# A linear-attention and SwiGLU kernel: the eps of the norm in a 385th column, another ring for 237 PSUM tiles, and a new order of its steps

## The chip, the cores and the metric

The kernel runs on one core of one Trainium2 chip. The metric is the device time of one execution in microseconds (us), as the median of several runs. A profile of one execution stands beside it; its times are from the span's start. In the profile, PE is TensorE, PEld its weight loads, DVE is VectorE, ACT is ScalarE, POOL is GpSimd and SP is SyncE, which here only issues DMA transfers (SPq).

## The reference

Batch 4, 8 heads, 768 tokens, 48 columns per head. The first half is a linear attention whose state decays per token and column; its output, 3072 rows of 384, goes through an RMS norm with a gain and a SwiGLU block of width 1536.

```python
for t in range(S):
    cur = np.einsum('bhd,bhe->bhde', u[None] * kt, vt)
    y[:, :, t] = np.einsum('bhd,bhde->bhe', rt, state + cur)
    state = wt[:, :, :, None] * state + np.einsum('bhd,bhe->bhde', kt, vt)
...
rms = np.sqrt(np.mean(x * x, axis=-1, keepdims=True) + 1e-06)
xn = x / rms * rms_g
g = xn @ w_gate
silu = g * (1.0 / (1.0 + np.exp(-g)))
val = xn @ w_val
return (silu * val @ w_out).astype(np.float32)
```

## The kernel before

Tokens are worked in blocks of 128. There are six blocks (n = 0 to 5) of four batches (j = 0 to 3). Blocks 0 and 1 are loaded together (384 KB for each input and batch) and handled as pairs of interleaved tokens; blocks 2 to 5 come in loads of 192 KB. Each piece of work is a small function, a step, called as `name.n.j`.

The steps of one block and batch, in the order of their data: `load_w`, `load_k`, `load_r`, `load_v` (SP, L248 for the first two blocks, L258 later); `ln` of the decay (ACT); running sums on PE (`cs_mm`, `cs_k`) and `cs_add` (DVE); `exp_r` and `exp_k` (ACT); the products `r_mul` (DVE) and `k_mul` (POOL L457, the "k product"); `bonus_mul`, two products on POOL (L464, L465), their sum `bonus_sum` (DVE L469) and `bonus_v` (POOL L475, the "v product"); the transpose of r and k, which blocks 0 and 1 do on PE (`rk_pe`, L482) with a copy on DVE or ACT (`rk_tr`), and blocks 2 to 5 by a transposing DMA on SP (`rk_tr`, L487); the score product `q_mm` (PE L501 to L515, two batches at a time from block 2 on), its masks `q_mask_e` and `q_copy_o`, and for some batches a select on POOL, `q_mask_o` (L536); `cast_v` (ACT or POOL L384); the state (`st_mm`, `st_new`) and the output `y_mm`; `x_add`, `x_sq` (L581), `x_rstd`, `xn_mul` for the norm; a transpose, `xn_pe` and `xn_out`, or for blocks 4 and 5 `xn_tr` (SP) and `xn_gain` (POOL L625). Then the block's feed-forward: twelve units each of `gate_mm` and `val_mm` (PE L646), `silu` (ACT), `h_mul` (DVE L666, the gating product), then `o_mm` (PE L683, the output product), `o_out` and `out_dma` (SP L707). `warm` (L377) is a dummy matmul on zeros.

POOL also issues the weight transfers, which cast on the way: `load_gv.1.0` and `load_gv.1.1` are eight of the twelve column blocks of the gate and the value weights (768 KB as they land), `load_gv.0.0` and `load_gv.0.1` the other four, and `load_wo` (L353) the output weights. The first value unit in both orders uses the large value transfer.

The order is written out: `ORDER` is a table of all steps, and every engine runs its own steps in the order in which they stand there. An engine that waits for one step holds all of its later steps. Sets of names (`CAST_ACT`, `XN_DVE`, `RK_DVE`, `ODD_DVE`, `RSTD_ACT`, `OUT_DVE`) choose the engine of single steps.

PSUM's eight banks are three rings: a (2 banks, default for gate units and running sums), b (2, value units) and q (4, all else). `psum()` (L225) takes in a ring the free bank whose last use in the table lies furthest back. ACT holds one of two tables of functions; `act()` (L234) puts a table load (L236) ahead of a step that needs the other one: logarithm and exponential, or silu.

Of the kernel before, what the change touches and what calls it, by code (L numbers as in the profile page):

```python
# [10 lines left out]
FP32 = mybir.dt.float32  # L11
# [25 lines left out]
bonus_v.1.0 exp_k.0.3 exp_r.0.3 y_mm.0.0 warm.23.0 q_mm.0.5 warm.24.0 warm.25.2 x_add.0.0 q_copy_o.0.5 y_mm.1.0
q_mask_o.0.5 cast_v.1.1 q_mask_e.0.5 cast_v.0.1 load_v.0.2 r_mul.0.2 x_sq.0.0 x_add.1.0 rk_pe.1.2 load_w.2.0
load_w.2.1 rk_tr.1.2 q_mm.0.1 warm.26.0 warm.27.0 warm.28.0 warm.29.2 q_copy_o.0.1 q_mask_e.0.1 exp_r.1.3 load_gv.1.1
q_mm.1.1 warm.30.2 x_rstd.0.0 st_mm.0.0 k_mul.0.2 w_tot.0.2 x_sq.1.0 q_mask_e.1.1 xn_mul.0.0 load_v.0.3 bonus_v.0.1  # L40
x_rstd.1.0 y_mm.0.1 rk_pe.0.2 q_copy_o.1.1 load_w.2.3 w_tot.0.3 xn_pe.0.0 st_new.0.0 xn_mul.1.0 x_add.0.1 cs_k.0.3
rk_tr.0.2 exp_k.1.3 xn_out.0.0 x_sq.0.1 bonus_mul.1.1 r_mul.0.3 xn_pe.1.0 warm.31.1 warm.32.2 xn_out.1.0 q_mm.1.5
warm.33.1 gate_mm.0.2 silu.0.2 gate_mm.0.3 silu.0.3 q_mask_o.1.1 q_mask_e.1.5 x_rstd.0.1 bonus_sum.1.1 q_copy_o.1.5
q_mm.1.2 r_mul.1.3 load_r.2.0 k_mul.1.3 bonus_v.1.1 bonus_mul.0.3 y_mm.1.1 xn_mul.0.1 x_add.1.1 gate_mm.0.5
gate_mm.0.4 q_mm.1.6 q_mask_e.1.2 load_gv.0.0 k_mul.0.3 q_copy_o.1.2 q_mask_e.1.6 silu.0.5 load_gv.0.1 bonus_mul.1.2
rk_pe.1.3 rk_tr.1.3 val_mm.0.3 xn_pe.0.1 xn_out.0.1 h_mul.0.3 q_copy_o.1.6 x_sq.1.1 val_mm.0.5 x_rstd.1.1 q_mm.1.7
# [87 lines left out]
def kernel(  # L134
# [610 lines left out]
```

## Time and profile before

| | us |
|---|---|
| median of 3 runs | 200.35 |
| lowest and highest of them | 199.78, 203.26 |
| span of the profiled execution | 197.6 |

The profiled execution is one execution by itself; what the page gives of it is its span, from the first to the last instruction. In the page, the share behind an engine is its busy time over the span. Of the transfers that the change moves, these are some (the last column is the median of us from issue to landing):

```profile
out_dram<-ob SPq DMA_DIRECT2D x19, 192.0 KB, 2.4
wt<-in_w_dram SPq DMA_DIRECT2D x16, 192.0 KB, 4.2
...
wt<-in_w_dram SPq DMA_DIRECT2D x4, 384.0 KB, 4.3
rt<-in_r_dram SPq DMA_DIRECT2D x4, 384.0 KB, 4.9
kt<-in_k_dram SPq DMA_DIRECT2D x4, 384.0 KB, 4.9
...
wo_sb<-in_moe_w_out_dram POOLq DMA_DIRECT2D x3, 384.0 KB, 7.1
```

A line such as `wt<-in_w_dram` reads "tile from tensor".

### The profile page before, as it was taken

Reading aid. Unit: us, or ns where it says so; the run is one execution under the profiler, and the core shown is the slowest. Engines: PE = TensorE matmul, PEld = TensorE weight load, DVE = VectorE, ACT = ScalarE, POOL = GpSimd, SP = SyncE. Lnnn points to the kernel's source line nnn. Section 1 sums busy time; section 2 is a strip of 40 time slices with the busy share of each in tenths; the row PEclk is TensorE's granted clock in tenths of the full one; section 3 lists DMA queues with packets and bytes.
Section 4 is the critical chain, followed back from the end, with each engine's and each line's share of the span. In section 5 each row is a group of like instructions: output and inputs, shape, how many; then the busy total and the mean of one; then the engine's idle time right before and its main releaser. Section 6 shows DMA issues by size and latency. Waiting matters only on the chain.

```text
span 197.6 us, 4751 instructions
## 1 busy us (share of the span) xinstructions
PE 191.5 (97%) x1742; PEld 120.4 (61%) x1742; DVE 156.4 (79%) x315; ACT 139.1 (70%) x286; POOL 127.5 (64%) x181
## 2 busy tenths in 40 slices
PE   7899999999999999999999999999999999999994
PEld 3456677888665556655655655666655655555563
DVE  5699998999997999989799988997689842435530
ACT  3989998979997889795699875698556760514201
POOL 3399999988599759793969998599661544000000
PEclk9999999999999999999999999999999999999999
DMA  6999999999897999999999967924580021012112
GB/s 164 320 325 267 244 220 205 220 213 197 174 230 162 199 179 214 200 211 214 185 206 225 202 147 166 227 51 145 134 216 12 5 60 60 20 63 80 40 60 101
DMA packets 109807, 32.42 MB, mean 164 GB/s; under 512 B 104276, under 2 KB 108632, under 8 KB 109784
## 3 DMA queue, kind: packets, MB, share of 16 engines
q1 hardware_dynamic: 107744, 28.58, 63.4%
q0 software_dynamic: 2032, 3.54, 10.0%
q8 instruction: 13, 0.21, 0.5%
q14 instruction: 10, 0.08, 0.1%
q10 hardware_dynamic: 8, 0.00, 0.0%
HBM read 25.96 MB, written 4.72 MB: 155 GB/s over the span
## 4 chain that ended last, share of the span: by engine, by line
PE 83%; DMA 7%; POOL 6%; SPq 1%; issue 1%; ACT 0%; POOLq 0%
PE ps_bu L646 13%; PE ps_bv L646 12%; PE ps_av L646 11%; PE ps_au L646 11%; PE ps_qv L683 7%; PE ps_qx L683 6%; PE ps_qz L683 6%; DMA wv_sb<-in_moe_w_val_dram 5%; PE ps_qu L683 5%; DMA kt<-in_k_dram 2%; POOL ruk L464 1%; POOL ruk L465 1%; SPq L248 1%; POOL qts L536 1%; PE ps_qz L513 1%
## 5 line engine op out<-in xcount | busy, mean ns | idle before, releaser
L238 ACT ACTIVATE sg<-ps_av 128x512 bf16<-128x512 f32 x36 | 21.5, 596 | 27.1 <-PE ps_av L646 21.4
L683 PEld LDWEIGHTS <-ht 128*128 128x128 bf16 x312 | 28.6, 98 | 18.3 <-DVE ht L666 0.4
L646 PEld LDWEIGHTS <-wg_sb 128*128 128x128 bf16 x252 | 27.0, 114 | 16.6 <-issue 0.3
L646 PEld LDWEIGHTS <-wv_sb 128*128 128x128 bf16 x252 | 26.4, 114 | 16.0 <-DMA wv_sb<-in_moe_w_val_dram 0.7
L666 DVE TENSOR_TENSOR ht<-ps_bu,sg 128x512 bf16<-128x512 f32 x37 | 25.4, 687 | 10.7 <-PE ps_bu L646 8.3
L666 DVE TENSOR_TENSOR ht<-ps_bv,sg 128x512 bf16<-128x512 f32 x35 | 24.0, 686 | 9.9 <-PE ps_bv L646 8.5
L646 PE MATMUL ps_bu<-xnt,wv_sb 128*128 128x512 bf16 (+1 forms) x135 | 30.3, 343 | 0.5 <-DMA wv_sb<-in_moe_w_val_dram 0.5
L646 PE MATMUL ps_av<-xnt,wg_sb 128*128 128x512 bf16 (+1 forms) x126 | 29.4, 350 | 0.0
L646 PE MATMUL ps_au<-xnt,wg_sb 128*128 128x512 bf16 (+1 forms) x126 | 29.3, 349 | 0.1
L646 PE MATMUL ps_bv<-xnt,wv_sb 128*128 128x512 bf16 (+1 forms) x117 | 28.5, 358 | 0.0
L464 POOL TENSOR_TENSOR ruk<-rt,kt 128x384 f32<-128x384 f32 x24 | 24.0, 1002 | 1.9 <-DVE diag L469 1.4
L465 POOL TENSOR_TENSOR ruk<-ruk,u_bc 128x384 f32<-128x384 f32 x24 | 24.0, 1000 | 1.9
L238 ACT ACTIVATE sg<-ps_au 128x512 bf16<-128x512 f32 x36 | 21.5, 596 | 4.5 <-PE ps_au L646 3.3
L457 POOL TENSOR_TENSOR rk<-kt,ek 128x384 bf16<-128x384 f32 x20 | 19.8, 1001 | 6.6 <-DMA kt<-in_k_dram 5.5
L475 POOL TENSOR_TENSOR ydiag<-vt,diag 128x384 f32<-128x384 f32 x24 | 19.9, 836 | 1.0 <-DVE diag L469 1.0
L236 ACT ACT_TABLE_LOAD x14 | 18.0, 1283 | 1.9 <-PEq L729 1.6
L536 POOL TENSOR_SCALAR_AFFINE_SELECT qts<-qts 128x512 bf16<-128x512 bf16 x19 | 11.9, 637 | 11.2 <-ACT qts L533 8.0
L683 PE MATMUL ps_qv<-wo_sb,ht 128*128 128x384 bf16 (+1 forms) x96 | 15.5, 311 | 0.0
L581 ACT ACTIVATE junk<-xb 128x384 bf16<-128x384 f32 x24 | 12.5, 521 | 4.2 <-DVE xb L576 3.9
L469 DVE TENSOR_REDUCE diag<-ruk 128x8 f32<-128x384 f32 x24 | 13.0, 544 | 0.0
L683 PE MATMUL ps_qx<-wo_sb,ht 128*128 128x384 bf16 x72 | 12.7, 326 | 0.0
L683 PE MATMUL ps_qz<-wo_sb,ht 128*128 128x384 bf16 x72 | 12.7, 326 | 0.0
(212 smaller groups left out, 376.8 us busy)
## 6 DMA issues: line engine op xcount, KB each, us to landing
out_dram<-ob SPq DMA_DIRECT2D x19, 192.0 KB, 2.4
wt<-in_w_dram SPq DMA_DIRECT2D x16, 192.0 KB, 4.2
rt<-in_r_dram SPq DMA_DIRECT2D x16, 192.0 KB, 4.4
vt<-in_v_dram SPq DMA_DIRECT2D x16, 192.0 KB, 3.7
kt<-in_k_dram SPq DMA_DIRECT2D x16, 192.0 KB, 4.0
wt<-in_w_dram SPq DMA_DIRECT2D x4, 384.0 KB, 4.3
rt<-in_r_dram SPq DMA_DIRECT2D x4, 384.0 KB, 4.9
kt<-in_k_dram SPq DMA_DIRECT2D x4, 384.0 KB, 4.9
```

The lines of the kernel that those rows point to most:

```text
L236: nc.scalar.preload_act_table_set(table_name)
L238: return nc.scalar.activation(**kw).ins
L457: eng.tensor_tensor(out=rk[:, n % 2, j, 1, :, 0:D], in0=inp["k", n, j], in1=bank["cs_k", n, j][:, 0:DM].rearrange("p (h d) -> p h d", h=H) ...
L464: eng.tensor_tensor(out=ruk[n, j], in0=inp["r", n, j], in1=inp["k", n, j], op=ALU.mult)
L465: eng.tensor_tensor(out=ruk[n, j], in0=ruk[n, j], in1=u_bc, op=ALU.mult)
L469: nc.vector.tensor_reduce(out=diag[n, j].rearrange("p h o -> p (h o)"), in_=ruk[n, j], axis=mybir.AxisListType.X, op=ALU.add)
L475: eng.tensor_tensor(out=ydiag[n, j], in0=inp["v", n, j], in1=diag[n, j].to_broadcast([128, H, D]), op=ALU.mult)
L536: nc.gpsimd.affine_select(out=qts[n, j][:, 1], in_=qts[n, j][:, 1], compare_op=ALU.is_ge if n < 2 and j // 4 < n else ALU.is_gt, fill=0.0, ...
L581: nc.scalar.activation(out=junk, in_=xb[n, j], func=AF.Square, accum_out=rstd[n, j][:, 0:1])
L646: nc.tensor.matmul(ps.rearrange("p (i t) -> p i t", t=cols.stop - cols.start)[:, i, :], lhsT=units(ws, c, fs.start + i), rhs=xnt[n][:, c, ...
L666: nc.vector.tensor_tensor(out=ht[n][:, fs, cols], in0=bank.pop(("v", n, f)).rearrange("p (i t) -> p i t", i=fs.stop - fs.start), in1=bank. ...
L683: nc.tensor.matmul(ps[:, cols], lhsT=ht[n][:, f, b * L:(b + 1) * L], rhs=wo_sb[:, f, cols], start=(f == 0), stop=(f == FC - 1))
```

## The change

Four things are done.

1. **The eps column.** The sum x that the norm works on was a tile of 384 columns. It now lies in one of four rows of `xrow`, each with a 385th column that is set once to sqrt(eps × 384). `x_sq` squares and sums 385 columns with a scale of 384^-0.5, so its sum is mean + eps, and `x_rstd` no longer scales or adds: on ACT its logarithm has neither scale nor bias, on POOL one of two instructions goes (L589).
2. **Rings by name.** 237 PSUM tiles are listed in `MOVED_Q` (99), `MOVED_A` (64) and `MOVED_B` (74) with the ring that they use instead of their default.
3. **The order and the sets.** `ORDER` is another table of the same steps, with 30 dummy matmuls instead of 34 and 21 selects instead of 19. Nineteen casts of v are on ACT instead of 13 (5 on POOL instead of 11); `XN_DVE` has 8 names instead of 6, `ODD_DVE` 11 instead of 13, `RSTD_ACT` 7 instead of 8, with the last norm (block 5, batch 2) among them, `OUT_DVE` 14 instead of 12. The table loads on ACT become 16 instead of 14.
4. **The gain.** `xn_gain` keeps only its POOL form, the one that was in use.

```diff
-rk_tr.1.0 bonus_sum.0.0 w_tot.0.0 load_gv.1.0 exp_r.1.1 load_r.0.2 q_mm.0.0 warm.16.0 q_mm.1.4 warm.17.1 warm.18.2
...
+load_k.0.2 bonus_mul.0.1 load_gv.1.0 bonus_sum.0.0 w_tot.0.2 x_sq.1.0 k_mul.0.2 bonus_v.0.0 warm.9.2 st_mm.0.0
...
+    moved = {}
+    for c, names in (("q", MOVED_Q), ("a", MOVED_A), ("b", MOVED_B)):
+        for x in names.split():
+            name, n, j = x.split(".")
+            moved[name, int(n), int(j)] = c
 
     def psum(ring, key, shape, dtype=FP32):
+        ring = moved.get(key, ring)
         slots = rings[ring]
...
+    xrow = const.tile([128, NXB, DM + 16], FP32)
+    nc.vector.memset(xrow[:, :, DM:DM + 1], (eps * DM) ** 0.5)
+    xlast = {(int(b), int(c)): i for i, (a, b, c) in enumerate(x.split(".") for x in ORDER.split())
+             if a in ("x_sq", "xn_mul")}
+    xslots = [[-2, i] for i in range(NXB)]
...
     def x_add(n, j):
-        xb[n, j] = pt.tile([128, DM], FP32, name="xb", bufs=NXB)
-        nc.vector.tensor_tensor(out=xb[n, j], in0=bank.pop(("y", n, j)),
+        k = min((x for x in range(NXB) if xslots[x][0] < at[0]), key=lambda x: xslots[x])
+        xslots[k] = [xlast[n, j], NXB + at[0]]
+        xb[n, j] = xrow[:, k, 0:DM + 1]
+        nc.vector.tensor_tensor(out=xb[n, j][:, 0:DM], in0=bank.pop(("y", n, j)),
                                 in1=ydiag[n, j].rearrange("p h d -> p (h d)"), op=ALU.add)
...
-        nc.scalar.activation(out=junk, in_=xb[n, j], func=AF.Square, accum_out=rstd[n, j][:, 0:1])
+        nc.scalar.activation(out=junk[:, 0:DM + 1], in_=xb[n, j], func=AF.Square, scale=DM ** -0.5,
+                             accum_out=rstd[n, j][:, 0:1])
...
-            act(LN_EXP, out=ss, in_=ss, func=AF.Ln, scale=1.0 / DM, bias=eps_col)
+            act(LN_EXP, out=ss, in_=ss, func=AF.Ln)
             act(LN_EXP, out=rstd[n, j][:, 1:2], in_=ss, func=AF.Exp, scale=-0.5)
         else:
-            nc.gpsimd.tensor_scalar(out=ss, in0=ss, scalar1=1.0 / DM, scalar2=eps, op0=ALU.mult, op1=ALU.add)
             nc.gpsimd.tensor_tensor(out=rstd[n, j][:, 1:2], in0=ss, in1=mhalf, op=ALU.pow)
```

The line numbers shift with the diff: L457 becomes L472, L464 and L465 become L479 and L480, L475 becomes L490, L536 becomes L551, L384 becomes L399, L350 becomes L358, L258 becomes L268, L487 becomes L502 and L707 becomes L720.

Two engines, POOL and SP, show what the new table moves at three places. The first is POOL, from its first k product to the transfer of the large gate weights (`wg_sb`). Before:

```order
L457 TENSOR_TENSOR rk<-kt,ek 128x8x48
L464 TENSOR_TENSOR ruk<-rt,kt 128x384
L465 TENSOR_TENSOR ruk<-ruk,u_bc 128x384
L464 TENSOR_TENSOR ruk<-rt,kt 128x384
L465 TENSOR_TENSOR ruk<-ruk,u_bc 128x384
L464 TENSOR_TENSOR ruk<-rt,kt 128x384
L465 TENSOR_TENSOR ruk<-ruk,u_bc 128x384
L457 TENSOR_TENSOR rk<-kt,ek 128x8x48
L350 DMA wg_sb_138<-in_moe_w_gate_dram 128x3x1024
```

The same stretch of POOL's queue in the changed kernel:

```order
L472 TENSOR_TENSOR rk<-kt,ek 128x8x48
L479 TENSOR_TENSOR ruk<-rt,kt 128x384
L480 TENSOR_TENSOR ruk<-ruk,u_bc 128x384
L479 TENSOR_TENSOR ruk<-rt,kt 128x384
L480 TENSOR_TENSOR ruk<-ruk,u_bc 128x384
L472 TENSOR_TENSOR rk<-kt,ek 128x8x48
L551 AFFINE_SELECT qts<-qts 128x512
L490 TENSOR_TENSOR ydiag<-vt,diag 128x384
L551 AFFINE_SELECT qts<-qts 128x512
L479 TENSOR_TENSOR ruk<-rt,kt 128x384
L480 TENSOR_TENSOR ruk<-ruk,u_bc 128x384
L358 DMA wg_sb_136<-in_moe_w_gate_dram 128x3x1024
```

Two selects and a v product have come ahead of the transfer, and the third pair of bonus products stands behind them. The next piece is POOL's queue from there to the transfer of the large value weights (`wv_sb`), before:

```order
L475 TENSOR_TENSOR ydiag<-vt,diag 128x384
L536 AFFINE_SELECT qts<-qts 128x512 x2
L475 TENSOR_TENSOR ydiag<-vt,diag 128x384
L536 AFFINE_SELECT qts<-qts 128x512
L384 CAST vb<-vt 128x384
L350 DMA wv_sb_140<-in_moe_w_val_dram 128x3x1024
```

And after:

```order
L472 TENSOR_TENSOR rk<-kt,ek 128x8x48
L490 TENSOR_TENSOR ydiag<-vt,diag 128x384
L479 TENSOR_TENSOR ruk<-rt,kt 128x384
L480 TENSOR_TENSOR ruk<-ruk,u_bc 128x384
L358 DMA wv_sb_138<-in_moe_w_val_dram 128x3x1024
```

Two v products, three selects and a cast have given way to a k product, a v product and a bonus pair. The last place is SP's queue up to the v load of block 3, batch 3 (the last row; before, it is the second of two v loads). The names are the input tiles, the output tile `ob` and the transposed tile `rkT`. Before:

```order
L258 DMA vt<-in_v_dram 128x8x48
L258 DMA kt<-in_k_dram 128x8x48
L258 DMA wt<-in_w_dram 128x8x48
L258 DMA kt<-in_k_dram 128x8x48
L258 DMA rt<-in_r_dram 128x8x48 x2
L258 DMA kt<-in_k_dram 128x8x48
L258 DMA wt<-in_w_dram 128x8x48
L258 DMA kt<-in_k_dram 128x8x48
L707 DMA out_dram<-ob 128x384
L258 DMA rt<-in_r_dram 128x8x48
L707 DMA out_dram<-ob 128x384
L258 DMA vt<-in_v_dram 128x8x48 x2
```

After, from the r load of block 3, batch 2, on:

```order
L268 DMA rt<-in_r_dram 128x8x48
L720 DMA out_dram<-ob 128x384
L502 DMA_TRANSPOSE rkT<-rk 128x8x128
L268 DMA rt<-in_r_dram 128x8x48
L268 DMA wt<-in_w_dram 128x8x48
L720 DMA out_dram<-ob 128x384
L502 DMA_TRANSPOSE rkT<-rk 128x8x128
L268 DMA kt<-in_k_dram 128x8x48
L720 DMA out_dram<-ob 128x384
L268 DMA kt<-in_k_dram 128x8x48
L502 DMA_TRANSPOSE rkT<-rk 128x8x128
L268 DMA vt<-in_v_dram 128x8x48
```

The v load now stands behind three transposes of block 3 and three stores. Counted from the transpose `rk_tr.2.2`, the entries ahead of it are 30 instead of 19, five of them transposes; the PE steps between the two places are nearly the same.

More of the change, by code (lines that the diff above doesn't have):

```diff
@@ L37 @@
[L37 to L46, printed above, removed]
@@ L130 @@
+out_dma.5.3
 """
@@ L325 @@
     nc.vector.memset(mhalf, -0.5)
-    eps_col = small.tile([128, 1], FP32)
-    nc.vector.memset(eps_col, eps)
     lw = persist.tile([128, 2, SB, H, PD], BF16)
@@ L382, in cast_v @@
             nc.scalar.copy(out=vb[n, j], in_=inp["v", n, j])
+        elif (n, j) in CAST_DVE:
+            nc.vector.tensor_copy(out=vb[n, j], in_=inp["v", n, j])
         else:
```

223 lines of the change are left out of this document (116 added, 107 removed).

## The prediction

> **What bounds the kernel now.** I read the profile's page first: busy time of each engine over the span, and the shares of the chain that ended last.
>
> ```profile
> span 197.6 us, 4751 instructions
> PE 191.5 (97%) x1742; PEld 120.4 (61%) x1742; DVE 156.4 (79%) x315; ACT 139.1 (70%) x286; POOL 127.5 (64%) x181
> ...
> PE 83%; DMA 7%; POOL 6%; SPq 1%; issue 1%; ACT 0%; POOLq 0%
> ```
>
> TensorE is busy for 97% of the span and carries 83% of the chain. The second reading is by stretches: start and end, length, then busy time (and count) of PE, weight loads, DVE, ACT and POOL, then the granted clock, the DMA share and GB/s.
>
> ```profile
> 5.00:25.80 20.80, 19.19 (x258) 11.93 (x257) 19.00 (x40) 19.28 (x42) 17.26 (x21) 1.00 1.16 289
> ...
> 30.80:60.00 29.20, 29.20 (x352) 23.79 (x353) 27.83 (x56) 26.66 (x55) 25.15 (x36) 1.00 1.05 203
> 60.00:155.00 95.00, 94.98 (x811) 56.00 (x809) 83.96 (x162) 72.02 (x152) 72.20 (x96) 1.00 0.79 171
> 155.00:194.70 39.70, 39.70 (x255) 23.03 (x251) 17.70 (x30) 14.14 (x31) 6.26 (x12) 1.00 0.17 53
> ```
>
> From 30.80 to 194.70 TensorE does not pause, at the full granted clock (1.00). So the end is the moment at which that unbroken run begins, plus the TensorE work left by then, plus every new pause. The third view is TensorE's waits (total us, times, longest), of which this one stands at the start of the run, and the fourth the chain in order of time around it, with a later output product.
>
> ```profile
> PE ps_bu L646 <- DMA wv_sb<-in_moe_w_val_dram: 0.5, 1, 0.5
> ```
>
> ```profile
> 8.18 1.00 POOL rk L457
> ...
> 16.17 0.99 POOL wg_sb L350
> ...
> 20.98 9.76 DMA wv_sb<-in_moe_w_val_dram
> 30.79 0.84 PE ps_bu L646 x6
> ...
> 73.64 1.95 PE ps_qx L683 x12
> ```
>
> The run begins with the first value matmul at 30.79. It is let go by the transfer of the value weights, issued by POOL at 20.98 and landed 9.76 later. POOL works its queue in order, from its first k product at 8.18 on, so the length of POOL's queue ahead of the two big weight transfers sets the start of the run.
>
> **The change part by part.**
>
> *Ahead of the first value matmul.* The steps that POOL does there are priced by these groups (busy us, mean ns of one):
>
> ```profile
> L464 POOL TENSOR_TENSOR ruk<-rt,kt 128x384 f32<-128x384 f32 x24 | 24.0, 1002 | 1.9 <-DVE diag L469 1.4 <-DMA kt<-in_k_dram 0.5
> L465 POOL TENSOR_TENSOR ruk<-ruk,u_bc 128x384 f32<-128x384 f32 x24 | 24.0, 1000 | 1.9
> L475 POOL TENSOR_TENSOR ydiag<-vt,diag 128x384 f32<-128x384 f32 x24 | 19.9, 836 | 1.0 <-DVE diag L469 1.0
> L457 POOL TENSOR_TENSOR rk<-kt,ek 128x384 bf16<-128x384 f32 x20 | 19.8, 1001 | 6.6 <-DMA kt<-in_k_dram 5.5 <-ACT ek L238 1.0
> L536 POOL TENSOR_SCALAR_AFFINE_SELECT qts<-qts 128x512 bf16<-128x512 bf16 x19 | 11.9, 637 | 11.2 <-ACT qts L533 8.0 <-DMA vt<-in_v_dram 3.2
> ```
>
> Before, eight rows lie between POOL's first k product and the gate weights: 16.17 − 8.18 = 7.99 us for 2 k products and 3 pairs of bonus products. After, eleven: the same eight (7.99), 2 selects (1.27) and one v product (0.84), 10.1 in all. The first k load moves one place up in SP's queue, where a load takes some 1.3 us, so POOL may start at 6.9, but not if its exponential comes later, which now heads ACT's queue with a different input. I let it start between 6.9 and 8.2, which gives the gate weights an issue between 17.0 and 18.3. From there to the value weights' issue lie the issue itself (0.99), a k product, a v product and a bonus pair: 0.99 + 1.00 + 0.84 + 2.00 = 4.8, as before (20.98 − 16.17 = 4.81). So the value weights are issued between 21.8 and 23.1 and, at 9.76, land between 31.6 and 32.9. I take 32.2.
>
> TensorE itself must be ready by then. Before, it waited 0.5 for that transfer, so it stood ready at 30.3. After, the same steps lie ahead of the first value matmul and two more, the transposes and the score product of one more block. Their prices come from starts in TensorE's own rows:
>
> ```profile
> 32.39 0.23 PE L501 MATMUL ps_qu<-rkT 48*128 48x128 bf16 x1
> 32.72 0.62 PE L482 MATMUL ps_qv<-ident,rk 128*128 128x128 bf16 x8
> 33.18 0.82 PE L646 MATMUL ps_bu<-xnt,wv_sb 128*128 128x256 bf16 x6
> ```
>
> That is 32.72 − 32.39 = 0.33 and 33.18 − 32.72 = 0.46, together 0.79: ready at 31.1. The run then begins at 32.2 with 0.79 less to do: 32.2 − 30.79 − 0.79 = **+0.6**. Bounds: 31.1 gives −0.5 (weights in time), 32.9 gives +1.3. The four dummy matmuls that go lie ahead of the run, where TensorE waits anyway: 0. Behind the value matmul VectorE is held too, since the gating product of that unit stands ahead of others in its queue. That costs nothing more, because TensorE would need those results only behind the same matmul.
>
> *The eps column, the casts, the tables.* Sixteen small POOL scalings go and six casts leave POOL for ACT. Both engines have room inside the run (72.02 and 72.20 of 95 us between 60 and 155), and ACT's square gets one column more in 385: 0. One more pair of table loads stands around the last norm (block 5, batch 2). A load and what follows it:
>
> ```profile
> 25.99 1.28 ACT L236 ACT_TABLE_LOAD   x1
> 27.28 0.60 ACT L238 ACTIVATE sg<-ps_au 128x512 bf16<-128x512 f32 x1
> ```
>
> It costs 1.28, and the next step starts 0.01 behind it. Between the last gate unit of block 4, whose silu is the last user of the other table, and the first gate unit of block 5, which needs the norm, TensorE has a value unit and four output products of 1.95, over 8 us, and ACT is idle for most of that stretch (14.14 of 39.70 busy). I take 0; the bound is the whole load, 1.3. The Trainium skill, "ScalarE: Activation LUTs", section "What ACT_TABLE_LOAD costs", puts a switch at 1283 ns plus a drain of about 1380 ns, 2.66 us in all. The load agrees with the row and the drain is not in it; by the page the bound would be 2.7 and the term still 0.
>
> *Inside the run.* The engines' totals hardly change, so what counts is what arrives late. The place where after's table leaves least is SP's queue between the transpose "rk_tr.2.2" and the v load of the fourth batch of block 3. SP's own rows, and the landing of r and v loads and of a transpose (last column, us from issue):
>
> ```profile
> 84.27 4.01 SPq L487 DMA_TRANSPOSE rkT<-rk  x3
> 88.33 1.20 SPq L258 DMA_DIRECT2D vt<-in_v_dram  x2
> ...
> 109.37 0.43 SPq L258 DMA_DIRECT2D kt<-in_k_dram  x1
> ```
>
> ```profile
> rt<-in_r_dram SPq DMA_DIRECT2D x16, 192.0 KB, 4.4
> vt<-in_v_dram SPq DMA_DIRECT2D x16, 192.0 KB, 3.7
> ...
> rkT<-rk SPq DMA_TRANSPOSE x16, 2.9
> ```
>
> Between 88.33 and 109.37 SP issued 23 plain transfers back to back: 21.04 / 23 = 0.91 each. A transpose takes 4.01 / 3 = 1.34. Before, 19 transfers stand from "rk_tr.2.2" to that v load; after, 30, five of them transposes: 25 × 0.91 + 5 × 1.34 = 29.4. One of the five waits besides: the r load of batch 2 comes after 17 plain ones and two transposes (18.2), lands 4.4 later, and POOL needs 2.0 and 1.0 for the bonus pair and the k product before the transpose "rk_tr.3.3" may go, at 25.6, where SP stands at 24.0. That is 1.6 more, 31.0. The v load then lands (3.7), ACT casts it (some 0.45, scaled by columns from the 0.60 of the silu above) and does the silu behind it (0.60), which frees the PSUM tile for the score product "q_mm.3.2": 35.8. How long TensorE has until then, and how far POOL runs ahead, can be read in before, at the k product that came earliest against its place:
>
> ```profile
> 85.73 1.00 POOL L457 TENSOR_TENSOR rk<-kt,ek 128x384 bf16<-128x384 f32 x1
> ```
>
> ```profile
> 87.74 0.81 PE L646 MATMUL ps_av<-xnt,wg_sb 128*128 128x512 bf16 x3
> 88.39 0.59 PE L646 MATMUL ps_bu<-xnt,wv_sb 128*128 128x512 bf16 x2
> ```
>
> A unit takes 88.39 − 87.74 = 0.65. TensorE's work between the two places is 25 gate and value units (16.3), 4 output products (7.8) and twenty smaller steps at about 0.3: 29.8. So if SP comes to "rk_tr.2.2" just at its place, TensorE waits 6.0 at the score product; every microsecond by which POOL's k product of that step is ahead of its place is taken off. The k product at 85.73 stands in the table behind the unit of 87.74 (end 88.55), so it came 2.8 early; others came at their places. After, POOL has only 7.8 us of work (three k products, two pairs, a v product) between the place of "exp_k.2.2", on which the step depends, and the step's own, against 13.5 us of TensorE's (16 units, an output product, three small steps): it can be up to 5.7 early. I take 4.4, about midway between 2.8 and 5.7, so **+1.6**; the bounds are 0 and 6.0.
>
> *The tail.* The last output piece is 192 columns wide instead of 96, so its copy takes longer:
>
> ```profile
> 194.74 0.24 ACT L692 COPY ob<-ps_qu 128x96 f32<-128x96 f32 x1 [0.54 <-PE ps_qu L683]
> ```
>
> With twice the columns I estimate +0.1 (bounds 0 and 0.24).
>
> **Sum.** 197.6 + 0.6 + 1.6 + 0.1 = 199.9 for the profiled execution. Its median time of the runs lies 200.35 − 197.6 = 2.75 above that span, which I add: 202.65, said as **202.6**.
>
> **The rivals.**
>
> *Nothing waits (chance 0.12).* The weights land by 31.1 and POOL runs its full 5.7 ahead, which leaves 0.3 at the score product. For it speaks that POOL loses work; against it, that its queue ahead of both transfers is longer. 197.6 − 0.5 + 0.3 + 0.1 = 197.5, so 200.25. This bounds the gain: before 25.80 ACT (19.28 of 20.80) and VectorE (19.00) are full, so TensorE cannot come to the value matmul several microseconds sooner, and a gain of 4 us has no row to come from: all that ACT has idle there is 1.5, which would make it 198.7. A chance of 0.05 stays for faster.
>
> *SP's queue is late (0.29).* POOL runs no further ahead than before, and the score product "q_mm.3.2" waits. For it: the k products of before were never over 2.8 early, and SP had no idle between 84 and 109. It decides from 2.6 early down: there the wait is 3.4, the span 197.6 + 0.6 + 3.4 + 0.1 = 201.7 and the time 204.4. At its place the wait is 6.0: 204.3, so 207.05. A second place would add to it: "k_mul.5.1" stands 0.65 of TensorE's work (one unit) ahead of the score product that needs it, where the product (1.0) and its transpose (2.9) take 3.9; before, no block from 2 on had less than 4.6 there. If POOL is at its place there too, that is 3.2 more, and 210.3. A pause of that length has a page against it: the Trainium skill, "TensorE: Matmul & The Clock Gate", section "What's actually happening", says that the clock falls to half after an idle window of about 3.4 us. No run here shows a pause so long, and the times above are without it.
>
> **How the numbers follow.** The forecast (late by 0 to 1.3 at the weights and by 0.3 to 3.4 in SP's queue, 200.3 to 204.4) has 0.54. My range leaves out the second place of the late queue and the gain: from the 198.7 of the first rival's best to the 207.1 of the second at its place. Two per cent of 200.35, about what a measurement tells from no change, is 196.3 and 204.4. Slower: 0.29 and a little of the forecast's upper end, 0.31. Faster 0.05. The rest, 0.64, within.
>
> **What would show it.** Right: the first value matmul at 31.6 to 32.9 waiting for its weights by 0.5 to 1.8; a wait of 0.3 to 3.4 at the score product of block 3, batches 2 and 3, led back to a late v load; POOL's wait for the r load before it; no wait at the last norm. Wrong: a value matmul before 31, or other waits in the run that sum to over 2 us.

## The result and the profile after

| | us |
|---|---|
| before, median of 4 runs (lowest and highest) | 200.06 (199.39 to 203.26) |
| after, median of 4 runs | 206.03 (204.94 to 208.33) |
| after over before | 1.0295, 95% interval 1.0241 to 1.0348 |
| the same two kernels again, medians of 6 and 10 runs | 206.0 and 199.16, ratio 1.0309 (1.0272 to 1.0346) |
| span of the profiled execution of after, and its own time | 206.6, 208.33 |

The changed kernel is 3% slower. Medians and ranges here are of all runs; the ratios leave out single slow executions, those that are over 1.5% above the fastest of their kernel. The profiled execution is the longest of its four; a profile of the repeat (span 204.9) shows the pauses at the same steps, three of them clearly shorter and one small one absent, so what follows doesn't rest on one execution. The page's busy times and the shares of the chain that ended last:

```profile
span 206.6 us, 4686 instructions
...
PE 190.9 (92%) x1721; PEld 121.1 (59%) x1738; DVE 157.9 (76%) x317; ACT 143.5 (69%) x290; POOL 123.3 (60%) x162
...
PE 43%; POOL 20%; DMA 15%; DVE 6%; ACT 5%; SPq 5%; issue 5%; POOLq 0%; DVEq 0%; ACTq 0%
```

TensorE's work is what it was (190.9 against 191.5; 17 matmul records are missing). The span grew by 9.0, and TensorE's share of the chain fell from 83% to 43%: POOL and DMA transfers took its place. By stretches (columns as before):

```profile
5.00:32.10 27.10, 23.21 (x333) 16.47 (x331) 24.33 (x50) 25.00 (x52) 23.55 (x29) 1.00 1.13 261
...
60.00:125.00 65.00, 59.23 (x495) 35.16 (x501) 52.74 (x105) 48.26 (x101) 43.94 (x55) 1.00 0.92 187
125.00:203.60 78.60, 77.13 (x560) 45.08 (x567) 51.92 (x93) 42.78 (x85) 30.42 (x39) 1.00 0.35 82
```

The same 65 us before:

```profile
60.00:125.00 65.00, 64.98 (x549) 37.87 (x547) 58.53 (x114) 52.09 (x109) 52.97 (x70) 1.00 0.94 194
```

Before, TensorE was busy without a gap from 30.80. Now 5.8 of the 65 us between 60 and 125 are idle, and VectorE, ACT and POOL do less there too: nothing is overloaded, everything is late. The granted clock stays at 1.00. TensorE's waits from 26 on (total us, times, longest):

```profile
PE ps_qz L659 <- DMA wg_sb<-in_moe_w_gate_dram: 1.8, 1, 1.8
PE ps_au L629 <- DVE st L567: 1.2, 1, 1.2
PE ps_qx L659 <- DVE ob L703: 1.2, 1, 1.2
PE ps_qu L696 <- DVE rk L466: 1.1, 1, 1.1
PE ps_bu L530 <- ACT sg L248: 1.0, 1, 1.0
PE ps_bu L586 <- POOL vb L399: 0.7, 1, 0.7
...
```

Before, this list had one row of 0.5. Now there are many small waits at five different lines, let go by VectorE, ACT and POOL as well as by transfers, mostly because the PSUM bank that a matmul wants is still being read. The next table has the gaps between TensorE's instructions behind 33 us. The place is the start of the matmul ahead of the gap. A gap is counted from the moment at which the next matmul could have started, as matmuls back to back do (0.22 us after the last one for 512 columns), so it comes out some 0.15 longer than the wait above, which counts from the modelled end. Gaps up to 0.22 are left out, since a missing record would leave one too.

| place | step that waits | us |
|---|---|---|
| 52.6, 53.6 | transpose, output product of block 0 | 0.23, 0.57 |
| 65.4 | second half of the first score product of block 2 | 0.27 |
| 73.5, 74.5 | output of block 2, batch 2 | 0.89, 0.56 |
| 84.4, 85.2 | transpose of block 2, output product | 0.25, 0.30 |
| 89.9, 91.9 | gate unit of block 2, state of block 2 | 1.34, 0.50 |
| 102.8 | score product "q_mm.3.2" | 1.16 |
| 116.8, 120.8 | transpose of block 3, output product | 1.38, 0.29 |
| 152.4 | output product of block 3 | 1.21 |

They sum to 8.95. With the 0.56 by which the run of TensorE's work starts later (below), that is 9.5, half a microsecond more than the 9.0 to be explained: no other loss has to be looked for. Who stands behind them is read from POOL's timeline (start, length, instruction, and in brackets how long POOL had been idle and what ended it):

```profile
72.88 0.50 POOL L399 CAST vb<-vt 128x384 bf16<-128x384 f32 x1 [2.63 <-DMA vt<-in_v_dram]
90.33 1.00 POOL L479 TENSOR_TENSOR ruk<-rt,kt 128x384 f32<-128x384 f32 x1 [5.97 <-DMA rt<-in_r_dram]
103.07 0.83 POOL L490 TENSOR_TENSOR ydiag<-vt,diag 128x384 f32<-128x384 f32 x1 [5.32 <-DMA vt<-in_v_dram]
113.11 1.00 POOL L479 TENSOR_TENSOR ruk<-rt,kt 128x384 f32<-128x384 f32 x1 [3.64 <-DMA kt<-in_k_dram]
```

Four loads, of block 2 ("load_v.2.3"), of block 3 ("load_r.3.2", "load_v.3.3") and of block 4 ("load_k.4.0"), come when POOL has been idle for 2.6 to 6.0 us. Three of them stand just ahead of TensorE's gaps (at 73.5, 102.8 and 116.8); the r load at 90.33 has none of its own but holds back the v load, as the chain below shows. Before, POOL waited for such loads by 3.2 in all between 60 and 118; after, by 18.4 (the four rows, and 0.8 for another r load). Why they come late is in SP's queue, in SP's timeline:

```profile
83.08 2.72 SPq L502 DMA_TRANSPOSE rkT<-rk  x1
85.90 0.53 SPq L720 DMA_DIRECT2D out_dram<-ob  x1
86.87 0.37 SPq L268 DMA_DIRECT2D rt<-in_r_dram  x1
...
96.51 2.71 SPq L502 DMA_TRANSPOSE rkT<-rk  x1
99.26 0.58 SPq L268 DMA_DIRECT2D vt<-in_v_dram  x1
```

The r load is issued at 86.87 and the v load at 99.26, each behind a transpose that holds SP for 2.7; the transposes at 88.04 and 93.38, in the same stretch, take 1.25. The long ones hold SP until a product on POOL is done (at 84.37 and 97.76 in the chain below) and then take their 1.4; and POOL waits for loads that stand behind them in SP's queue. The chain that ended last shows the whole loop (start, us, what):

```profile
83.40 0.97 POOL rk L472
84.37 1.43 SPq L502
...
86.87 3.33 DMA rt<-in_r_dram
90.33 1.00 POOL ruk L479
...
92.40 1.92 POOL rk L472 x2
...
96.74 1.02 POOL ruk L480
97.76 1.45 SPq L502
99.26 3.68 DMA vt<-in_v_dram
103.07 0.83 POOL ydiag L490
...
109.31 3.73 DMA kt<-in_k_dram
113.11 1.01 POOL ruk L479
...
146.59 5.17 DMA vt<-in_v_dram
```

A k product on POOL lets a transpose go on SP, behind it an r load is issued, that lets POOL go on to its bonus products and the next k products, these let the next transpose go, and so on to the v load of block 3 and the k load of block 4. From 81 to 116 no TensorE work is among the long pieces of the chain. The load at 146.59 is "load_v.5.1", which lies behind transposes and stores in the same way; ACT's cast of it at 151.79 stands ahead of a VectorE product that holds a bank, and the output product at 153.86 waits 1.21.

### The profile page after: what moved, and what is told of

Same layout as the page of the kernel before. It is cut to its first block, busy times and chain, and to the rows that moved or that the text cites. A ratio compares the mean times of both kernels' runs of the same rounds, so it can differ in the third digit from the quotient of the medians.

```text
span 206.6 us, 4686 instructions
## 1 busy us (share of the span) xinstructions
PE 190.9 (92%) x1721; PEld 121.1 (59%) x1738; DVE 157.9 (76%) x317; ACT 143.5 (69%) x290; POOL 123.3 (60%) x162
## 4 chain that ended last, share of the span: by engine, by line
PE 43%; POOL 20%; DMA 15%; DVE 6%; ACT 5%; SPq 5%; issue 5%; POOLq 0%; DVEq 0%; ACTq 0%
DMA wv_sb<-in_moe_w_val_dram 5%; POOL ruk L479 5%; POOL ruk L480 5%; PE ps_qz L659 4%; DMA vt<-in_v_dram 4%; PE ps_bv L659 4%; PE ps_qv L659 4%; PE ps_au L659 3%; PE ps_qx L659 3%; PE ps_qu L659 3%; POOL rk L472 3%; PE ps_bu L659 3%; POOL ydiag L490 3%; POOL qts L551 2%; SPq L268 2%
## 5 line engine op out<-in xcount | busy, mean ns | idle before, releaser
L479 POOL TENSOR_TENSOR ruk<-rt,kt 128x384 f32<-128x384 f32 x24 | 24.1, 1002 | 10.5 <-DMA rt<-in_r_dram 6.8
L490 POOL TENSOR_TENSOR ydiag<-vt,diag 128x384 f32<-128x384 f32 x24 | 19.8, 832 | 10.6 <-DMA vt<-in_v_dram 5.3
L472 POOL TENSOR_TENSOR rk<-kt,ek 128x384 bf16<-128x384 f32 x20 | 20.0, 1007 | 9.4 <-ACT ek L248 9.2
L480 POOL TENSOR_TENSOR ruk<-ruk,u_bc 128x384 f32<-128x384 f32 x24 | 24.0, 1001 | 1.9
L607 POOL TENSOR_TENSOR rstd<-rstd,mhalf 128x1 f32<-128x1 f32 x17 | 9.3, 552 | 13.2 <-ACT junk L598 12.8
L598 ACT ACTIVATE junk<-xrow 128x385 bf16<-128x385 f32 x24 | 12.7, 527 | 4.7 <-DVE xrow L593 4.5
L551 POOL TENSOR_SCALAR_AFFINE_SELECT qts<-qts 128x512 bf16<-128x512 bf16 x21 | 13.3, 637 | 2.4 <-ACT qts L548 1.5
L248 ACT ACTIVATE lw<-wt 128x384 bf16<-128x384 f32 (+1 forms) x20 | 11.7, 588 | 2.2 <-DMA wt<-in_w_dram 2.1
L395 ACT CAST vb<-vt 128x384 bf16<-128x384 f32 x19 | 9.6, 514 | 4.5 <-DMA vt<-in_v_dram 4.5
L659 PE MATMUL ps_qu<-xnt,wv_sb 128*128 128x512 bf16 (+1 forms) x43 | 10.5, 351 | 0.1
L248 ACT ACTIVATE sg<-ps_au 128x512 bf16<-128x512 f32 x12 | 7.2, 597 | 4.5 <-PE ps_au L659 3.0
L659 PE MATMUL ps_qv<-xnt,wg_sb 128*128 128x256 bf16 (+1 forms) x47 | 9.8, 326 | 0.1
L659 PE MATMUL ps_au<-xnt,wg_sb 128*128 128x512 bf16 (+1 forms) x42 | 9.7, 335 | 0.2
L614 ACT ACTIVATE xn<-xrow,rstd 128x384 bf16<-128x384 f32 x16 | 9.5, 608 | 0.1
L679 DVE TENSOR_TENSOR ht<-ps_bv,sg 128x512 bf16<-128x512 f32 x9 | 6.1, 682 | 4.1 <-PE ps_bv L659 4.1
```

What stands on the lines that cost most here:

```text
L248: return nc.scalar.activation(**kw).ins
L472: eng.tensor_tensor(out=rk[:, n % 2, j, 1, :, 0:D], in0=inp["k", n, j], in1=bank["cs_k", n, j][:, 0:DM].rearrange("p (h d) -> p h d", h=H) ...
L479: eng.tensor_tensor(out=ruk[n, j], in0=inp["r", n, j], in1=inp["k", n, j], op=ALU.mult)
L480: eng.tensor_tensor(out=ruk[n, j], in0=ruk[n, j], in1=u_bc, op=ALU.mult)
L490: eng.tensor_tensor(out=ydiag[n, j], in0=inp["v", n, j], in1=diag[n, j].to_broadcast([128, H, D]), op=ALU.mult)
L551: nc.gpsimd.affine_select(out=qts[n, j][:, 1], in_=qts[n, j][:, 1], compare_op=ALU.is_ge if n < 2 and j // 4 < n else ALU.is_gt, fill=0.0, ...
```

## The experiments

Theory A: the order of SP's queue brings a few loads late, and the engines' queues carry the lateness to banks that TensorE wants. Its rivals: B, the ring lists put tiles in banks that come free late; C, stores that are late in SP's queue hold the three output buffers, and these hold banks; D, the eps column and the tables on ACT; E, the weights at the start. In kernels made from the changed one by moved steps the line numbers are smaller by one.

**The parts alone.** The eps column alone, put into the kernel before (order, rings and sets of before):

```diff
-        nc.scalar.activation(out=junk, in_=xb[n, j], func=AF.Square, accum_out=rstd[n, j][:, 0:1])
+        nc.scalar.activation(out=junk[:, 0:DM + 1], in_=xb[n, j], func=AF.Square, scale=DM ** -0.5,
+                             accum_out=rstd[n, j][:, 0:1])
...
-            act(LN_EXP, out=ss, in_=ss, func=AF.Ln, scale=1.0 / DM, bias=eps_col)
+            act(LN_EXP, out=ss, in_=ss, func=AF.Ln)
```

> The kernel before with the eps column alone (x in rows of 385 columns, no scaling step on POOL, no bias on ScalarE); order, sets and rings as before. My forecast gave this edit 0: 199.5 to 200.6. If POOL's 16 small steps mattered to the path, it is faster by 1 to 3 us; if the wider square or the shared rows hold ScalarE, slower by 1 or more.

Measured: 199.16 against 199.71, ratio 0.9979 (0.9947 to 1.0012). No difference: this half of D falls.

The changed kernel with the ring lists passed over; each tile takes, of all eight banks, the one whose last use lies furthest back:

```diff
-        ring = moved.get(key, ring)
+        ring, k = min(((r, x) for r in "abq" for x in range(len(rings[r])) if rings[r][x][0] < at[0]),
+                      key=lambda y: rings[y[0]][y[1]])
         slots = rings[ring]
-        k = min((x for x in range(len(slots)) if slots[x][0] < at[0]), key=lambda x: slots[x])
```

> The changed kernel with the lists of rings put aside: every PSUM tile takes, among all eight banks, the one whose last use in the table lies furthest back. Theory B: the five pauses in which TensorE waits for VectorE or ScalarE to empty a bank go, 200 to 202.5. Theories A and C: the readers of the banks are late whichever bank it is, 204 to 207.

Measured: 206.53 (206.28 to 207.37), ratio 1.0346 (1.028 to 1.0413), as slow as the changed kernel. TensorE's waits are then named on other banks (the longest, 1.5, on "ps_bv" instead of "ps_qx", again behind an output copy), and POOL's on the loads are 5.9, 4.8 and 3.2. A bank that is read late is late whichever it is. B falls as far as this shows: the lists of after cost nothing against the freest choice. The default rings alone under the new order were not tried.

A fourth output buffer:

```diff
-        ob = pt.tile([128, DM], FP32, name="ob", bufs=3)
+        ob = pt.tile([128, DM], FP32, name="ob", bufs=4)
```

> The changed kernel with four output buffers instead of three. In its trace VectorE waited 1.0 and 1.7 us around 88 and 90 us for a buffer whose store was queued on SP, and a gate unit waited 1.3 us for that copy's bank. If the stores are a cause of their own beside the loads: 1 to 2 us faster than the changed kernel, 203.5 to 205. If SP's late loads carry the time and this wait only lies beside them: 205 to 206.5.

Measured: 206.63 (206.03 to 208.11), ratio 1.0357 (1.0305 to 1.0408). In the changed kernel two output copies on VectorE do wait for a store:

```profile
88.07 0.56 DVE L703 COPY ob<-ps_au 128x384 f32<-128x384 f32 x1 [0.98 <-DMA out_dram<-ob]
90.82 0.56 DVE L703 COPY ob<-ps_qx 128x384 f32<-128x384 f32 x1 [1.73 <-DMA out_dram<-ob]
```

With the fourth buffer these waits and the gap of 1.34 behind them are gone, and the gap at the score product is 2.09 instead of 1.16 (0.35 in the repeat). The gating product that starts at 93.08 in the repeat starts at 90.62 here, so TensorE was 2.5 ahead; the one just behind the score product starts at 104.12 in the repeat and at 103.98 here. The v load was issued at 97.63 instead of 98.67, earlier by only 1.0, and nearly all of the lead was lost at it. Not all of the lead is the buffer's: the gaps of 1.3 at block 2's output are gone as well, since that v load landed at 71.36 instead of 72.23.

The time of 206.63, though, can't settle what the buffer is worth. The mean granted clock was 0.983 to 0.992 in all four executions, against 0.998 to 1.000 in the repeat. The profiled one shows where (columns as in the stretches above):

```profile
25.20:28.60 3.40, 1.59 (x26) 1.38 (x23) 2.63 (x6) 3.05 (x5) 3.38 (x5) 1.00 1.15 228
28.60:32.00 3.40, 3.40 (x28) 2.41 (x26) 1.15 (x2) 1.98 (x5) 1.88 (x3) 0.50 1.14 198
100.30:103.70 3.40, 1.48 (x20) 0.86 (x20) 1.45 (x3) 2.04 (x6) 1.94 (x3) 1.00 1.00 198
103.70:107.10 3.40, 3.18 (x9) 1.20 (x9) 1.29 (x2) 1.73 (x5) 3.32 (x6) 0.50 1.05 210
```

Twice the clock stood at 0.50 for 3.4 us, the second time right behind the score product. Half the clock for 3.4 us is up to 1.7 us of TensorE's work, an estimate. So C is real as a wait, and what it removed was lost again at the next late load; that it is worth nothing by itself is not shown, and up to a microsecond or two stays open. The stores stand in the same SP queue as the loads: with five loads moved (below) VectorE still waits 1.4 for a store, and TensorE has no gap behind it.

**Moving loads.** Where the loads stand in SP's queue, counted in entries from its start, in each kernel (bold: moved):

| load | before | changed | one moved | five moved | five, v further up | mirror |
|---|---|---|---|---|---|---|
| load_v.2.1 | 23 | 42 | 42 | **36** | **33** | 23 |
| load_v.2.3 | 36 | 43 | 43 | **37** | **34** | 36 |
| load_r.3.2 | 49 | 60 | **44** | **44** | **44** | **52** |
| load_v.3.3 | 57 | 71 | 71 | 71 | 71 | **62** |
| load_k.4.0 | 68 | 81 | 81 | **75** | **75** | **75** |
| load_v.5.1 | 96 | 105 | 105 | **95** | **95** | 96 |

All six stand 7 to 19 entries further back in the changed kernel than before. One of them first, "load_r.3.2" (16 entries earlier, where the expectation below says eight):

```diff
-q_mask_o.2.1 load_w.5.2 load_r.3.1
+q_mask_o.2.1 load_r.3.2 load_w.5.2 load_r.3.1
...
-gate_mm.2.5 load_r.3.2 exp_r.3.3
+gate_mm.2.5 exp_r.3.3
```

> The changed kernel with one step moved: the r load of block 3, batch 2 stands eight places earlier in SP's table order, ahead of the w load of block 5, batch 2. Theory A (SP's queue brings loads late, POOL waits for them and the pauses follow): POOL's wait of 6.0 us for that load goes, the 1.2 pause at the score product of block 3 shrinks by more than half, and the time falls by 1 to 3 us from 205.2 to 206.0, to 202.5 to 205. Theory B (the new rings reuse banks too early): nothing changes, 205 to 206. Theory C (POOL's own queue is too long, with or without loads): the wait for that load only moves to the next POOL step, 204.5 to 206.

Measured: 204.25 (202.72 to 206.28), ratio 1.0192 (1.0112 to 1.0272). POOL's waits for loads between 60 and 118 fall from 18.4 to 8.2, and TensorE's from 34 on are:

```profile
PE ps_bu L628 <- ACT xn L613: 1.3, 1, 1.3
PE ps_qu L695 <- DVE rk L465: 1.0, 1, 1.0
...
```

The wait at the score product is gone with one load, though the v load that it waited for was not moved: the r load had held it back. The transpose at 83.7 now waits longer (a gap of 1.44 instead of 0.25). The gaps at block 2's output are gone too, but not by the edit: its v loads are issued at 66.88 here and at 67.18 in the changed kernel, and POOL has the second of them at 70.93 instead of 72.88. That place is at the edge, and the transfer's own time decides it.

Then the other four as well:

```diff
-k_mul.2.3 bonus_sum.2.0 rk_tr.2.0
+k_mul.2.3 bonus_sum.2.0 load_v.2.1 load_v.2.3 rk_tr.2.0
...
-exp_r.4.0 load_r.4.0
+exp_r.4.0 load_k.4.0 load_r.4.0
...
-h_mul.3.6 cast_v.4.1 rk_tr.4.2
+h_mul.3.6 cast_v.4.1 load_v.5.1 rk_tr.4.2
```

> The changed kernel with five loads earlier in the table: r of block 3 batch 2, v of block 2 batches 1 and 3, k of block 4 batch 0, v of block 5 batch 1; all other steps stand as they did. Theory A: the pauses of 1.4 us at the output of block 2, 1.4 at the norm of block 3 and 1.2 at the output product of block 3 go too; 199.5 to 202.5, and POOL's waits for loads between 60 and 115 us fall from 18 us to under 6. Theory B: 204.5 to 206. Theory C: 203 to 206.

Measured: 202.22 (201.26 to 202.68), ratio 1.011 (1.0052 to 1.0169). POOL's waits for loads between 60 and 118 are 5.9. What is left of TensorE's waits from 34 on begins with this one, and a wait of 0.7 for gate weights follows:

```profile
PE ps_qv L527 <- DMA rkT<-rk: 0.9, 1, 0.9
...
```

The one shown is new: the two v loads now stand in front of the transpose "rk_tr.2.0", and the first score product of block 2 waits for it (a gap of 1.10 instead of 0.27). So the two v loads were put further up, ahead of "load_v.2.0":

```diff
-exp_k.2.0 xn_out.0.2 load_v.2.0
+exp_k.2.0 xn_out.0.2 load_v.2.1 load_v.2.3 load_v.2.0
```

> As the run with five loads earlier, but the v loads of block 2, batches 1 and 3, stand three places earlier still, ahead of the other v loads of that block, so that they no longer push a transpose back. Theory A: the pause of 1.1 us at the first score product of block 2 shrinks, 200.8 to 202. If that pause comes from the exponentials of block 2 (VectorE and ScalarE before 62 us) it stays, 201.7 to 202.6.

Measured: 202.02 (201.32 to 202.66), ratio 1.0108 (1.0067 to 1.015), no better; the gap at that score product is still 0.71, nearer to the second of the two expectations than to A's. Whether block 2's exponentials make it was not tested. The stretch from 60 to 125 is nearly filled again, at the same clock:

```profile
60.00:125.00 65.00, 63.45 (x541) 37.71 (x549) 57.63 (x113) 51.11 (x107) 49.06 (x60) 1.00 1.00 206
```

TensorE does 4.2 more work in it than after did (63.45 against 59.23). Five moved loads, no other change, took 4.0 us off (206.0 in the repeat, on the same chip, to 202.02).

**The mirror.** The same lateness put into the kernel before: three loads set back behind block 3's work or directly ahead of their use.

```diff
-ln.3.1 bonus_v.2.2 load_r.3.2 x_sq.2.0
+ln.3.1 bonus_v.2.2 x_sq.2.0
...
-cs_mm.3.2 ln.3.3 bonus_mul.3.2
+cs_mm.3.2 ln.3.3 load_r.3.2 bonus_mul.3.2
...
-load_v.3.1 load_v.3.3 cs_add.3.3
+load_v.3.1 cs_add.3.3
...
-h_mul.2.8 x_add.3.3 load_k.4.0 bonus_v.3.2
+h_mul.2.8 x_add.3.3 bonus_v.3.2
...
-x_sq.3.3 xn_mul.3.0 bonus_mul.4.0
+x_sq.3.3 xn_mul.3.0 load_k.4.0 bonus_mul.4.0
```

("load_v.3.3" goes directly ahead of "load_v.3.2".)

> The kernel before with three loads later and nothing else: r of block 3 batch 2 and k of block 4 batch 0 directly ahead of their first use in the table, v of block 3 batch 3 behind the transposes of block 3. Theory A: POOL waits 5 us or more for loads between 75 and 115 us where it waited 0.5, pauses appear in TensorE's run, 201.5 to 205. If late loads alone cannot do it (theories B and C): 199.5 to 200.6.

Measured: 201.44 (200.94 to 207.22), ratio 1.0105 (1.0069 to 1.0142). TensorE's waits from 26 on, then POOL's for the three loads:

```profile
PE ps_av L410 <- DVE wcol L447: 1.2, 1, 1.2
...
```

```profile
POOL vb L384 <- DMA vt<-in_v_dram: 3.1, 1, 3.1
POOL ruk L464 <- DMA kt<-in_k_dram: 2.7, 1, 2.7
...
POOL ruk L464 <- DMA rt<-in_r_dram: 0.9, 1, 0.9
```

POOL waits 6.7 for the moved loads and TensorE has two new gaps, 1.32 at 108.1 and 0.41 at 122.5: with everything else as before, late loads alone slow the kernel by 1%. The chain leads from the k load issued at 101.21 over POOL to the second of the gaps. The time lies just under what A expected (201.5 to 205).

**The start.** The two large weight transfers one bonus pair earlier on POOL, on top of the five loads:

```diff
-load_k.0.2 bonus_mul.0.1 load_gv.1.0 bonus_sum.0.0
+load_k.0.2 load_gv.1.0 bonus_mul.0.1 bonus_sum.0.0
...
-st_new.0.0 bonus_mul.1.1 r_mul.1.2
+st_new.0.0 load_gv.1.1 bonus_mul.1.1 r_mul.1.2
```

> As the run before it, and POOL issues the large gate and value transfers one bonus pair earlier each. My forecast's start term: the value weights land 2 us or more earlier, the first value matmul starts at 31.0 to 31.4 when TensorE is ready instead of 31.8, and the gate unit that waited 0.7 for the small gate transfer does not wait: 0.7 to 1.4 us faster than the run before it. If the weights do not set that start, or the bonus pairs are missed later, 0 or slower.

Measured: 202.04 (201.58 to 209.77), ratio 1.0107 (1.0064 to 1.0149): no gain, though the transfers are issued 2.0 earlier (15.52 and 20.28 instead of 17.52 and 22.28). TensorE now waits 1.4 for one of VectorE's k products a little ahead of the value matmul and only 0.2 for the weights: two things end at about the same time there.

Two masks moved from POOL to VectorE instead ("q_mask_o.0.2" and "q_mask_o.1.6" go), on top of the five loads:

```diff
-    ODD_DVE = sel("00 03 04 12 13 15 20 41 43 50 52")
+    ODD_DVE = sel("00 02 03 04 12 13 15 16 20 41 43 50 52")
```

> As the run with the v loads of block 2 three places earlier (five loads moved in all), and two selects of blocks 0 and 1 taken from POOL, done by VectorE's masking product instead, as in the kernel before. What is left over the kernel before there is 2 to 2.5 us, with pauses of 0.6 at 53.6 and 0.7 at 65.4. If POOL's longer list in the first 50 us (it waits for nothing between 35 and 49) is behind them, they shrink by half or more and the time falls by 0.6 to 1.3 us, to 200.4 to 201.5. If VectorE, which is as full there, is: no gain or up to 0.7 slower.

Measured: 202.02 (201.07 to 203.08), ratio 1.0128 (1.0095 to 1.0161): no gain; TensorE waits 1.0 for the mask on VectorE. And both together:

> As the run before it, and the two large weight transfers one bonus pair earlier. If both the start and POOL's first 50 us are what is left: 199.6 to 200.8, no more than 0.6 per cent over the kernel before. If the gain of the start is again lost at the score product of block 2: 200.8 to 202.

Measured: 201.37 (200.69 to 210.23), ratio 1.0093 (1.0065 to 1.012), still not before's time. The interval overlaps that of the five loads alone, so a gain from it isn't shown.

**The last norm.** On top of the five loads, the root of block 5's last norm goes back to POOL, where before has it; the table loads on ACT fall from 16 to 14:

```diff
-    RSTD_ACT = sel("00 03 10 23 32 33 52")
+    RSTD_ACT = sel("00 03 10 23 32 33")
```

> As the run with five loads moved, but the last norm's root (block 5, batch 2) on POOL again, so that the pair of table loads around it goes (14 loads instead of 16). My forecast gave the pair 0: no change, within 0.5 us of 202.0. If it showed at the end: 1 to 2.7 us faster.

Measured: 205.92 (204.6 to 206.21), ratio 1.0308 (1.0276 to 1.0341), a miss: 3.9 slower than with the root on ACT. POOL's timeline shows the reason for 2.2 of it:

```profile
169.16 2.39 POOL L640 TENSOR_TENSOR xnt<-xnt,gT 128x384 bf16<-128x384 bf16 x3 [3.26 <-DMA xnt<-xn]
171.51 0.55 POOL L606 TENSOR_TENSOR rstd<-rstd,mhalf 128x1 f32<-128x1 f32 x1
175.08 0.83 POOL L640 TENSOR_TENSOR xnt<-xnt,gT 128x384 bf16<-128x384 bf16 x1 [3.03 <-DMA xnt<-xn]
```

In this order the small root (0.55) stands behind three gains that wait for a transposing transfer, so its own transpose starts late and TensorE waits 2.1 for the last gain. The other half of D falls with the sign reversed: with the root on ACT, and the extra pair of table loads around it, TensorE has no gap at that norm, and the root's place on ACT is one of the things the new order needs. The gap at that place (2.25) is all of what the profiled execution (span 202.9) has over the one with five loads moved (200.7). The median of the runs lies 1.7 further up. The other three executions have spans of 204.1 to 204.5 and a mean granted clock of 0.989 to 0.990, against 1.00 in the profiled one; half the clock for some 3.4 us, as with the fourth buffer, would be about 0.8% of such a span, an estimate. No profile of them shows it.

**The repeat.** The changed kernel once more, five rounds:

> The changed kernel as it is, in five rounds and with a second trace, since its first four runs spread over 204.9 to 208.3. All theories: 205 to 206.5. Theory A says besides that the pauses of the run (TensorE silent behind 33 us) stand again behind late loads, at the output of block 2, at the score product of block 3 and at the norm of block 3, with sizes that may differ by a microsecond, and that POOL waits 10 us or more for r, k and v loads between 60 and 115 us.

Measured: 206.0 (204.53 to 206.64), ratio 1.0309 (1.0272 to 1.0346). Its profile (span 204.9) has the same gaps: among them 1.39 at the gate unit and 1.42 at the transpose of block 3, but 0.35 at the score product instead of 1.16, and 0.64 instead of 1.21 at block 3's output product. With the small one at 52.7 (0.23) all of them sum to 7.3. POOL's waits named on loads are 10.1 between 60 and 118 (6.4 for r, 3.7 for k), which is as little as theory A allowed. The two others, 2.6 ahead of the cast at 72.29 and 4.5 ahead of the v product at 101.92, end here with TensorE and VectorE, and the chain between 86.90 and 101.92 runs over a store of an output buffer and VectorE: where the r load and the store are both late, either can end last.

## Why the prediction was wrong

The forecast was 202.6 and most likely no clear change (0.64); the result was 206.0, slower. It lies inside the range, at the time of the second rival ("SP's queue is late", 204.4 to 207.05), which had 0.29. Two rows of the changed kernel's profile show how far ahead SP ran at the start of that queue: the transpose "rk_tr.2.2", and the matmuls behind which it stands in the table (the next unit starts at 68.68).

```profile
65.53 1.61 SPq L502 DMA_TRANSPOSE rkT<-rk  x1
```

```profile
68.04 0.81 PE L659 MATMUL ps_au<-xnt,wv_sb 128*128 128x512 bf16 x3
```

Point by point:

- *The start* held. The value weights were issued at 21.77 (forecast 21.8 to 23.1), took 10.33 and let TensorE go at 32.14 (forecast 32.2): +0.56 net of the 0.79 of work done ahead (forecast +0.6). Not foreseen was the wait of 1.8 for the gate weights at 27.56; it moved wait from the one place to the other and cost nothing of its own.
- *The score product "q_mm.3.2"* was the right place and the right path: a late v load, and POOL waiting for the r load ahead of it. That its wait came out near the forecast (1.16, and 0.35 in the repeat, for 1.6) is luck. By the two rows above, SP came to the transpose 3.2 ahead of its place, not 4.4 (POOL's k product was about 4.5 ahead of its own, as taken). From there to the v load's issue SP took 33.7, not 31.0, and the score product followed 4.8 later, as taken. TensorE's work between was 30.3 (29.8 in the forecast, whose terms make 30.1). That is 33.7 + 4.8 − 30.3 − 3.2 = 5.0 of lateness instead of 1.6. It shows as 1.16 only because TensorE had already lost 3.84 in the six gaps between 73 and 92.
- *The eps column, the extra pair of table loads and the tail* were put at 0, 0 and 0.1. The first was measured as none (0.9979), the second leaves no gap at the last norm; behind the last matmul stand 2.9 us in both profiles.
- *The step that failed* is "The place where after's table leaves least is SP's queue between the transpose "rk_tr.2.2" and the v load of the fourth batch of block 3", with its term of +1.6. It was too small at that place, and it was taken for the only place. By the score product 5.0 was lost instead of 1.6, spread over seven gaps. Behind it the same queue brought "load_k.4.0" and "load_v.5.1" late, at 116.8, 120.8 and 152.4, for 2.9 where the sum has nothing; the gaps at 52.6, 53.6 and 65.4 (1.1) were not in it either, and their cause is open. The r load was in the working, but only as a term (1.6) in SP's own sum; that POOL stands idle for 6.0 meanwhile, and that its v products, casts and selects queue behind that, was not followed to VectorE and the banks. The moved loads show late loads as the cause of about two thirds: they took off 4.0 us where the changed kernel was slower by 6.0 (6.8 in the repeat), and three late loads alone cost the kernel before 1%.
- *The rival* had the right cause, and with 3.4 to 6.0 nearly the right size for what was lost by the score product (5.0). It expected it in one wait there; it came in seven, and 2.9 came behind.
- *The offset* was mis-sized. The forecast added 2.75 from span to time, the median's distance from a span that belongs to another run. Wherever a run has its own span, they lie 1.7 apart (206.6 and 208.33, 204.9 and 206.64). With that the forecast would have been 201.6, and its true miss is 4.4.
- *The test that it set itself*, "other waits in the run that sum to over 2 us", is what came.

What stays open is the last 2 us (1.0108 with the loads moved). In the profile with five loads moved (span 200.7) they are the start (0.5) and gaps at 52.6 and 53.6 (0.80), 65.4 (0.71) and 83 to 88 (1.03), which makes 3.0 of its 3.1 over before; which choice of the new order makes each wasn't settled. No version found is faster than before.

## What to carry to other kernels

When a program is in order on every engine and its bound engine has no slack, ask of a new order, for every load, where its issue stands against its first reader, and not only where the queue is worst: one late queue takes its toll at each of its readers, and an in-order reader passes it on to steps that have nothing to do with the load. A load queue that also carries steps which wait for compute (here transposes and stores) can close a loop with the engine that computes for them; loads for the next block belong ahead of those steps. A wait that is removed ahead of a later wait on the same queue can be lost there again (of a lead of 2.5 us in the run with a fourth buffer 0.1 was left behind the next late load), so a better test of a cause is to move what is late than to add buffers where it shows. And the granted clock of every run has to be read before two times are compared.

## What the runs showed of the hardware

- The large gate transfer (768 KB) took 8.4 from issue to landing in before and 10.5 in after, the value transfer behind it 9.8 and 10.3.
- The same load (192 KB) issued at nearly the same moment landed some 2 us apart in two kernels ("load_v.2.3", issued at 67.80 and 67.51, landed at 72.83 and 70.87), which makes places with so little room a matter of the single execution.
- A transposing transfer's issue held SP for 1.25 where its data was ready and 2.7 where it wasn't (88.04 and 83.08), and the loads behind it waited for that.
- TensorE's granted clock stayed at 1.00 in the changed kernel's profile with its gaps of up to 1.8, and in the profile of the last norm with a gap of 2.25. In the profile of the fourth buffer it fell to 0.50 for 3.4 us twice, each time right behind 3.4 us in which TensorE was busy for 1.59 and 1.48. With 1.69 (changed kernel, 24.1 to 27.5) and 1.31 (last norm, 172.6 to 176.0) it did not fall. So neither figure alone tells whether it falls, and it fell behind gaps well under the 3.4 us that the prediction's second rival took as the condition.
